# Unequal units at the two ends of a software pipeline, weights loaded after the first gate, and input tiles moved to multiples of 512 B

## The chip, the cores and the metric

The kernel runs on one core of one Trainium2 chip. The metric is the device time in microseconds (us). The core has six units that matter here: TensorE (PE in the profile; PEld is its weight load), VectorE (DVE), ScalarE (ACT), GpSimd (POOL), SyncE (SP, here only an issuer of transfers) and 16 DMA engines.

A reported time is about 2 us longer than the span of the profile of the same run (237.56 against 235.8 us for the profiled run of the kernel before). Each run also lists the mean clock that TensorE was granted. The times of one kernel move a little with it: the kernel before took 235.8 us in a run at 0.998, 236.2 at 0.992 and 237.7 at 0.984. I therefore say the clock where a difference of one us matters.

## The reference

Four sequences of 6336 steps, 256 channels: a gated recurrence, then a highway layer on its result.

```python
sig = 1 / (1 + exp(-f_logit));  f = lb + (1 - lb) * sig;  i = 1 - f
h = f[:, t] * h + i[:, t] * x[:, t]          # for t in 0..6335; y[:, t] = h
H = maximum(y @ w_h, 0);  T = 1 / (1 + exp(-(y @ w_t + b_t)))
out = T * H + (1 - T) * y
```

Inputs and outputs are float32. 52.4 MB are read and 25.9 MB written, in whatever way the work is cut.

## The kernel before

The time axis is cut into *units* of columns, a column being one step of one sequence. A unit of 1024 columns is one sequence's piece of 1024 steps; the first unit holds the 192 odd steps of all four sequences (768 columns, on 96 partitions). The units go through a software pipeline, one unit per iteration `n`:

```python
rest = S % (NB * P)                                     # 192
units = [(rest // 2, [(b, 0, b * rest, rest) for b in range(B)])]   # 768 columns
for s0 in range(rest, S, NB * P):
    for b in range(B):
        units.append((P, [(b, s0, 0, NB * P)]))         # 24 units of 1024 columns
...
outp = ctx.enter_context(tc.tile_pool(name="outp", bufs=2))
...
for n in range(-3, NU + 2):
    load(n + 4)                       # SyncE: lt (f_logit) and xt (x)
    z_pe(n - 1, 0); scan(n, 0)        # TensorE; VectorE: y = f*y + b
    t_act(n - 1, 0)                   # ScalarE: t = sigmoid(z)
    o_pe(n - 2, 0); o_act(n - 2, 0)   # TensorE; ScalarE copy o, SyncE output
    decay_pe(n + 1, 0); decay_act(n + 1, 0)   # transposes uT; ScalarE f
    d_dve(n - 1, 0)                   # VectorE d
    ...                               # the same for the second half of channels
    gate(n + 2)                       # ScalarE: u = sigmoid(-f_logit)
    ...
    after = e_dve(n - 1)              # VectorE e = d*t
    product(n + 2, after)             # GpSimd: bv = u*x, held until e is done
# (cut: ok(n) guards, second halves)
```

So one iteration holds the VectorE work of unit `n` (scan) and of unit `n-1` (d, e), and the ScalarE work of units `n+2` (gate), `n+1` (f), `n-1` (t) and `n-2` (copy). Each of the matmul results has a single buffer in PSUM.

## Time and profile before

| | before |
|---|---|
| time, median of the first 3 runs | 236.1 us (235.98 to 236.21) |
| VectorE busy | 203.6 us, 86% of the span |
| ScalarE busy | 198.3 us, 84% |
| TensorE busy | 192.1 us, 81% |
| first scan | 16.48 us |
| one 1024-column unit | 8.19 us |
| end of the last e to the end of the span | 9.0 us |

The page of the kernel before: the span, the busy times, three rows of the 40 slices (digits are tenths, 9 is 90% or more; PEclk is the granted clock), and the chain of waits by engine.

```profile
span 235.8 us, 4853 instructions
PE 192.1 (81%) x2000; PEld 134.5 (57%) x2000; DVE 203.6 (86%) x144; ACT 198.3 (84%) x176; POOL 114.2 (48%) x108
...
DVE  0425799999999999999999999999999999999540
...
PEclk9999999999999999999999999999999999999985
DMA  6999999999999999999999999999999995243255
...
DVE 77%; issue 6%; PE 5%; ACT 2%; DVEq 0%; ACTq 0%
```

VectorE is full from the sixth slice to the last but three; the chain that ended last is 77% VectorE. Only the two ends have room. The timeline of VectorE shows them (columns: start, duration, engine, line, operation, result and operands, shapes, count; in brackets the idle time before and what ended it).

```profile
16.48 1.89 DVE L161 TENSOR_TENSOR_SCAN y<-f,bT 128x192 bf16<-128x192 f16 x4 [5.92 <-PE bT L150]
19.76 1.89 DVE L161 TENSOR_TENSOR_SCAN y<-f,bT 128x192 bf16<-128x192 f16 x4 [1.39 <-PE bT L150]
22.90 2.35 DVE L161 TENSOR_TENSOR_SCAN y<-f,y,bT 128x1024 bf16<-128x1024 f16 x1 [1.26 <-ACT u L119]
...
27.54 2.35 DVE L161 TENSOR_TENSOR_SCAN y<-f,y,bT 128x1024 bf16<-128x1024 f16 x1 [1.39 <-ACT t L183]
...
31.65 2.34 DVE L161 TENSOR_TENSOR_SCAN y<-f,y,bT 128x1024 bf16<-128x1024 f16 x1
...
224.16 1.28 DVE L199 SCALAR_TENSOR_TENSOR d<-y,ncc,gp 128x1024 bf16<-128x1024 bf16 x1 [2.55 <-PE gp L190]
225.55 1.23 DVE L206 TENSOR_TENSOR e<-d,t 128x2048 bf16<-128x2048 bf16 x1
```

Nothing is scanned for 16.5 us, three gaps of 1.3 to 1.4 us follow at the start and one of 2.55 us before the last d, and after the last e (which ends at 226.8) two copies and the last outputs take 9 us more.

Here the granted clock of TensorE falls to half from 228 us on (columns: stretch, its length, then PE, PEld, DVE, ACT, POOL busy with their counts, granted clock, DMA share, GB/s):

```profile
228.00:230.00 2.00, 1.01 (x10) 1.01 (x10) 0.00 (x0) 0.94 (x1) 0.00 (x0) 0.54 0.26 92
230.00:232.00 2.00, 0.85 (x8) 0.58 (x6) 0.00 (x0) 1.01 (x1) 0.00 (x0) 0.50 0.69 245
```

The last 16 matmuls of 128 columns take 308 ns on average there, where those before them took 220.

### The profile page before, as it was taken

Reading aid. Unit: us, or ns where it says so; the run is one execution under the profiler, and the core shown is the slowest. Engines: PE = TensorE matmul, PEld = TensorE weight load, DVE = VectorE, ACT = ScalarE, POOL = GpSimd, SP = SyncE. Lnnn points to the kernel's source line nnn. Section 1 sums busy time; section 2 is a strip of 40 time slices with the busy share of each in tenths; the row PEclk is TensorE's granted clock in tenths of the full one; section 3 lists DMA queues with packets and bytes.
Section 4 is the critical chain, followed back from the end, with each engine's and each line's share of the span. In section 5 each row is a group of like instructions: output and inputs, shape, how many; then the busy total and the mean of one; then the engine's idle time right before and its main releaser. Section 6 shows DMA issues by size and latency. Waiting matters only on the chain.

```text
span 235.8 us, 4853 instructions
## 1 busy us (share of the span) xinstructions
PE 192.1 (81%) x2000; PEld 134.5 (57%) x2000; DVE 203.6 (86%) x144; ACT 198.3 (84%) x176; POOL 114.2 (48%) x108
## 2 busy tenths in 40 slices
PE   0135899898999989899998989898999989897751
PEld 0125566666566666667566666656666666665441
DVE  0425799999999999999999999999999999999540
ACT  0645789999999999999999999999999999975541
POOL 1088553574376357436634753673475357430000
PEclk9999999999999999999999999999999999999985
DMA  6999999999999999999999999999999995243255
GB/s 150 302 386 386 386 383 386 379 385 383 382 386 383 386 382 386 384 384 379 386 386 382 385 383 383 379 382 375 385 383 386 388 368 205 97 152 119 89 178 177
DMA packets 78805, 78.68 MB, mean 334 GB/s; under 512 B 2240, under 2 KB 78784, under 8 KB 78784
## 3 DMA queue, kind: packets, MB, share of 16 engines
q1 hardware_dynamic: 77664, 77.86, 94.4%
q10 hardware_dynamic: 1120, 0.53, 0.9%
q8 instruction: 15, 0.25, 0.4%
q14 instruction: 6, 0.05, 0.0%
HBM read 52.43 MB, written 25.95 MB: 332 GB/s over the span
## 4 chain that ended last, share of the span: by engine, by line
DVE 77%; issue 6%; PE 5%; ACT 2%; DVEq 0%; ACTq 0%
DVE y L161 45%; DVE d L199 20%; DVE e L206 12%; PE zp L175 1%; PE gp L190 1%; ACT o L233 1%; ACT t L183 1%; PE op L224 1%; PE op L223 1%; PE bT L150 0%; PE uT L136 0%; DVE e L209 0%; DVEq L206 0%; ACTq L233 0%; DVEq L209 0%
## 5 line engine op out<-in xcount | busy, mean ns | idle before, releaser
L126 POOL TENSOR_TENSOR bv<-u,xt 128x512 bf16<-128x512 f16 (+1 forms) x100 | 113.2, 1164 | 93.7 <-DVE e L206 72.9
L161 DVE TENSOR_TENSOR_SCAN y<-f,y,bT 128x1024 bf16<-128x1024 f16 x48 | 112.3, 2341 | 2.6 <-ACT t L183 1.4
L183 ACT ACTIVATE t<-zp,bt 128x1024 bf16<-128x1024 f32 (+1 forms) x50 | 55.3, 1106 | 13.6 <-PE zp L175 10.6
L199 DVE SCALAR_TENSOR_TENSOR d<-y,ncc,gp 128x1024 bf16<-128x1024 bf16 (+1 forms) x50 | 62.2, 1244 | 2.5 <-PE gp L190 2.5
L144 ACT ACTIVATE f<-uT,ncc 128x1024 f16<-128x1024 f16 (+1 forms) x50 | 55.9, 1117 | 5.5 <-PE uT L136 5.5
L233 ACT COPY o<-op 128x1024 f32<-128x1024 f32 (+1 forms) x50 | 50.2, 1005 | 5.7 <-PE op L224 5.7
L190 PE MATMUL gp<-y,w_sb 128*128 128x512 bf16 (+1 forms) x200 | 51.5, 380 | 4.0 <-DVE d L199 1.4
L223 PE MATMUL op<-diag,y 128*128 128x128 f16 (+1 forms) x400 | 50.9, 221 | 2.2 <-ACT o L233 2.2
L175 PE MATMUL zp<-y,w_sb 128*128 128x512 bf16 (+1 forms) x200 | 51.6, 381 | 0.3 <-ACT t L183 0.3
L224 PE MATMUL op<-ident_b,e 128*128 128x128 bf16 (+1 forms) x400 | 50.8, 221 | 0.5 <-DVE e L206 0.5
L119 ACT ACTIVATE u<-lt 128x2048 f16<-128x2048 f32 (+1 forms) x25 | 47.5, 1902 | 2.1 <-DMA lt<-in_f_logit_dram 2.1
L150 PE MATMUL bT<-ident_b,bv 128*128 128x128 bf16 (+1 forms) x400 | 31.7, 222 | 20.8 <-DVE y L161 16.5
L224 PEld LDWEIGHTS <-e 128*128 128x128 bf16 (+1 forms) x400 | 39.7, 100 | 8.8 <-DVE e L206 1.9
L223 PEld LDWEIGHTS <-y 128*128 128x128 bf16 (+1 forms) x400 | 39.8, 100 | 5.7
L150 PEld LDWEIGHTS <-bv 128*128 128x128 bf16 (+1 forms) x400 | 26.8, 99 | 27.5 <-issue 20.0
L136 PE MATMUL uT<-ident_h,u 128*128 128x128 f16 (+1 forms) x400 | 32.2, 227 | 11.0 <-ACT u L119 10.0
L190 PEld LDWEIGHTS <-w_sb 128*128 128x128 f16 x200 | 19.6, 98 | 24.4 <-issue 7.1
L136 PEld LDWEIGHTS <-u 128*128 128x128 f16 (+1 forms) x400 | 26.0, 103 | 11.4 <-ACT u L119 10.0
L206 DVE TENSOR_TENSOR e<-d,t 128x2048 bf16<-128x2048 bf16 x24 | 29.4, 1225 | 2.9 <-DVE d L199 0.5
L175 PEld LDWEIGHTS <-w_sb 128*128 128x128 f16 x200 | 18.7, 99 | 18.2 <-issue 1.1
L161 DVE TENSOR_TENSOR_SCAN y<-f,bT 128x192 bf16<-128x192 f16 x8 | 3.8, 534 | 7.3 <-PE bT L150 7.3
L119 ACT ACT_TABLE_LOAD x1 | 1.3, 1283 | 6.7 <-DMA lt<-in_f_logit_dram 6.7
(15 smaller groups left out, 5.7 us busy)
## 6 DMA issues: line engine op xcount, KB each, us to landing
lt<-in_f_logit_dram SPq DMA_DIRECT2D x24, 1024.0 KB, 9.3
xt<-in_x_dram SPq DMA_DIRECT2D x24, 1024.0 KB, 10.6
out_dram<-o SPq DMA_DIRECT2D x48, 512.0 KB, 7.9
lt<-in_f_logit_dram SPq DMA_DIRECT2D x2, 384.0 KB, 5.0
xt<-in_x_dram SPq DMA_DIRECT2D x2, 384.0 KB, 5.7
out_dram<-o SPq DMA_DIRECT2D x2, 384.0 KB, 6.6
w_raw<-in_moe_w_h_dram ACTq DMA_DIRECT2D x1, 256.0 KB, 4.8
w_raw<-in_moe_w_t_dram ACTq DMA_DIRECT2D x1, 256.0 KB, 5.4
```

What stands on the lines that cost most here:

```text
L126: ins = pin(nc.gpsimd.tensor_mul(bv[:np_, q:q + 2], st[n]["u"][:np_, q:q + 2], st[n]["xt"][:np_, q:q + 2]))
L136: pin(nc.tensor.transpose(uT[:, j * np_:(j + 1) * np_], st[n]["u"][:np_, j, h * P:(h + 1) * P], ident_h[:np_, :np_]))
L144: pin(nc.scalar.activation(st[n]["f"][:, h, :N], st[n]["uT"][:, :N], AF.Identity, scale=ncc[:, h:h + 1], bias=1.0))
L150: pin(nc.tensor.transpose(bT[:, j * np_:(j + 1) * np_], st[n]["bv"][:np_, j, h * P:(h + 1) * P], ident_b[:np_, :np_]))
L161: pin(nc.vector.tensor_tensor_scan(y[:, h, c0:c0 + ln], st[n]["f"][:, h, c0:c0 + ln], st[n]["bT"][:, c0:c0 + ln], 0.0 if prev is None else ...
L175: pin(nc.tensor.matmul(zp[:, i, :e - a], w_sb[:, 1, ki, m * P:(m + 1) * P], y[:, ki, a:e], start=ki == 0, stop=ki == NH - 1))
L183: pin(nc.scalar.activation(st[n]["t"][:, m, :, :w], st[n]["zp"][:, :, :w], AF.Sigmoid, bias=bt[:, m:m + 1]))
L190: pin(nc.tensor.matmul(gp[:, i, :e - a], w_sb[:, 0, ki, m * P:(m + 1) * P], y[:, ki, a:e], start=ki == 0, stop=ki == NH - 1))
L199: pin(nc.vector.scalar_tensor_tensor(st[n]["d"][:, m, :, :w], y2, ncc[:, m:m + 1], st[n]["gp"][:, :, :w], op0=ALU.mult, op1=ALU.max))
L206: ins = pin(nc.vector.tensor_mul(e, st[n]["d"], st[n]["t"]))
L223: pin(nc.tensor.matmul(o, y[:, h, j * np_:(j + 1) * np_], diag[:, h], start=True, stop=False))
L224: pin(nc.tensor.matmul(o, e[:, h, i, c:c + np_], ident_b, start=False, stop=True))
```

## The change

The intent: start the scan sooner with a small first unit, keep the last unit short so that little stands behind its e, get the weights out of the way of the first loads, and let the input tiles start at multiples of 512 B.

- Units: 256 columns (64 steps of four sequences, loaded as two halves of 64 partitions), 512 (128 steps of four), 512 + 512, then 22 of 1024, and 512 + 256 + 256 for the last one. 29 units instead of 25, the same 25,344 columns.
- The weights (0.5 MB) are loaded by ScalarE after the first gate instead of at its very start; the VectorE work on them stands between the scans of the first two units.
- A small activation at the top loads ScalarE's table before the data come (1.28 us; in the kernel before from 6.71, when lt had landed). Its tile, `warm`, is 256 B a partition; the first input tile moves from 48.5 x 512 B to 49 x 512 B.

```diff
+    FIRST, LAST = (4, 4), (4, 2, 2)
-    units = [(rest // 2, [(b, 0, b * rest, rest) for b in range(B)])]
+    units.append((2, [(b, b * H, H) for b in range(B)],
+                  [(b0, slice(b0, B, 2), 0, b0 * H) for b0 in range(2)]))
+    units.append((4, [(b, b * P, P) for b in range(B)], [(0, slice(0, B), H, 0)]))
...
+            for nb in (LAST if last else FIRST if not b and s0 == H + P else (NB,)):
+                units.append((nb, [(b, 0, nb * P)], [(b, a)]))
+                a += nb * P
...
+    warm = singles.tile([P, 64], FP32, name="warm")
+    nc.gpsimd.memset(warm, 0.0)
+    nc.scalar.activation(warm, warm, AF.Sigmoid)
...
+    def load_weights():
+        for k, w in enumerate((moe_w_t, moe_w_h)):
+            pin(nc.scalar.dma_start(w_raw[:, 1 - k], w.rearrange("(h p) o -> p h o", p=P)))
...
         if ok(n):
             scan(n, 1)
+        if n == 0:
+            weights()
...
+        if n + 2 == 0:
+            load_weights()
```

(Every helper takes the unit's own width instead of a fixed one; e is one instruction for every unit; the output of a unit of up to 512 columns is one copy.)

More of the change, by code (lines that the diff above doesn't have):

```diff
@@ L42 @@
     NB = 8
+    FIRST, LAST = (4, 4), (4, 2, 2)
     out_bsd = out.rearrange("(b s) d -> b s d", b=B)
-    rest = S % (NB * P)
-    assert rest % 2 == 0 and rest // 2 <= P and B * 2 == NB
-    units = [(rest // 2, [(b, 0, b * rest, rest) for b in range(B)])]
-    for s0 in range(rest, S, NB * P):
-        for b in range(B):
-            units.append((P, [(b, s0, 0, NB * P)]))
+    units = []
+    H = P // 2
+    assert S % (NB * P) == H + P and B == 4
+    units.append((2, [(b, b * H, H) for b in range(B)],
+                  [(b0, slice(b0, B, 2), 0, b0 * H) for b0 in range(2)]))
+    units.append((4, [(b, b * P, P) for b in range(B)], [(0, slice(0, B), H, 0)]))
+    for s0 in range(H + P, S, NB * P):
+        for b in range(B):
+            last = s0 + NB * P == S and b == B - 1
+            a = s0
+            for nb in (LAST if last else FIRST if not b and s0 == H + P else (NB,)):
+                units.append((nb, [(b, 0, nb * P)], [(b, a)]))
+                a += nb * P
     NU = len(units)
@@ L65, in pin, with pieces @@
         return tc.keep_in_program_order(ins)
+    def pieces(n, dram, t):
+        nb, _, parts = units[n]
+        if len(parts[0]) == 2:
+            b, a = parts[0]
+            return [(dram[b, a:a + nb * P, :].rearrange("(j p) d -> p j d", p=P), t[:, :nb])]
+        w = H if len(parts) == 2 else P
+        return [(dram[bs, a:a + w, :].rearrange("b p d -> p b d"), t[p0:p0 + w, :nb]) for _, bs, a, p0 in parts]
     def load(n):
-        np_, segs = units[n]
         lt = inp.tile([P, NB, D], FP32, tag="lt")
@@ L71, in load @@
         for src, t in ((f_logit, lt), (x, xt)):
-            if len(segs) == 1:
-                b, s0, _, ln = segs[0]
-                pin(nc.sync.dma_start(t, src[b, s0:s0 + ln, :].rearrange("(j p) d -> p j d", p=np_)))
-            else:
-                t4 = t.rearrange("p (b j) d -> p b j d", j=2)
-                for j in range(2):
-                    nc.sync.dma_start(
-                        t4[:np_, :, j, :],
-                        src[:, j * np_:(j + 1) * np_, :].rearrange("b p d -> p b d"))
-        st[n]["lt"], st[n]["xt"] = lt, xt
+            for dram, sb in pieces(n, src, t):
+                pin(nc.sync.dma_start(sb, dram))
+        st[n]["lt"], st[n]["xt"] = lt, xt
+    warm = singles.tile([P, 64], FP32, name="warm")
+    nc.gpsimd.memset(warm, 0.0)
+    nc.scalar.activation(warm, warm, AF.Sigmoid)
+    lb = singles.tile([P, NH], FP32, name="lb")
+    bt = singles.tile([P, NH], FP32, name="bt")
+    w_raw = singles.tile([P, 2, NH, D], FP32, name="w_raw")
+    nc.scalar.dma_start(lb, lower_bound.rearrange("(h p) -> p h", p=P))
     load(0)
@@ L89 @@
     make_identity(nc, ident_h)
-    lb = singles.tile([P, NH], FP32, name="lb")
-    bt = singles.tile([P, NH], FP32, name="bt")
-    w_raw = singles.tile([P, 2, NH, D], FP32, name="w_raw")
-    for h in range(NH):
-        for vec, t in ((lower_bound, lb), (moe_b_t, bt)):
-            nc.scalar.dma_start(t[:, h:h + 1], bass.AP(
-                tensor=vec.tensor, offset=vec.offset + h * P, ap=[[1, P], [1, 1]]))
-    for k, w in enumerate((moe_w_h, moe_w_t)):
-        nc.scalar.dma_start(w_raw[:, k], w.rearrange("(h p) o -> p h o", p=P))
     cc = singles.tile([P, NH], FP32, name="cc")
@@ L107, with weights @@
     for h in range(NH):
-        for k in range(2):
-            nc.vector.tensor_scalar(w_sb[:, k, h], w_raw[:, k, h], cc[:, h:h + 1], None, op0=ALU.mult)
         nc.vector.tensor_scalar(diag[:, h], ident_h, cc[:, h:h + 1], None, op0=ALU.mult)
         nc.vector.tensor_scalar(ndiag[:, h], ident_h, ncc[:, h:h + 1], None, op0=ALU.mult)
-        nc.vector.scalar_tensor_tensor(w_sb[:, 0, h, h * P:(h + 1) * P], w_raw[:, 0, h, h * P:(h + 1) * P],
-                                       cc[:, h:h + 1], ndiag[:, h], op0=ALU.mult, op1=ALU.add)
+    def load_weights():
+        for k, w in enumerate((moe_w_t, moe_w_h)):
+            pin(nc.scalar.dma_start(w_raw[:, 1 - k], w.rearrange("(h p) o -> p h o", p=P)))
+        pin(nc.scalar.dma_start(bt, moe_b_t.rearrange("(h p) -> p h", p=P)))
+    def weights():
+        for h in range(NH):
+            pin(nc.vector.tensor_scalar(w_sb[:, :, h], w_raw[:, :, h], cc[:, h:h + 1], None, op0=ALU.mult))
+            pin(nc.vector.scalar_tensor_tensor(
+                w_sb[:, 0, h, h * P:(h + 1) * P], w_raw[:, 0, h, h * P:(h + 1) * P], cc[:, h:h + 1], ndiag[:, h],
+                op0=ALU.mult, op1=ALU.add))
     def gate(n):
-        np_, _ = units[n]
+        nb = units[n][0]
         u = inp.tile([P, NB, D], FP16, tag="u")
-        pin(nc.scalar.activation(u[:np_], st[n]["lt"][:np_], AF.Sigmoid, scale=-1.0))
+        pin(nc.scalar.activation(u[:, :nb], st[n]["lt"][:, :nb], AF.Sigmoid, scale=-1.0))
         st[n]["u"] = u
     def product(n, after):
-        np_, _ = units[n]
         bv = mid.tile([P, NB, D], BF16, tag="bv")
-        for q in range(0, NB, 2):
-            ins = pin(nc.gpsimd.tensor_mul(bv[:np_, q:q + 2], st[n]["u"][:np_, q:q + 2], st[n]["xt"][:np_, q:q + 2]))
+        for q in range(0, units[n][0], 2):
+            ins = pin(nc.gpsimd.tensor_mul(bv[:, q:q + 2], st[n]["u"][:, q:q + 2], st[n]["xt"][:, q:q + 2]))
             if q == 0 and after is not None:
@@ L132, in decay_pe @@
     def decay_pe(n, h):
-        np_, _ = units[n]
         uT = ps1.tile([P, NB * P], FP16, tag="uT")
-        for j in range(NB):
-            pin(nc.tensor.transpose(uT[:, j * np_:(j + 1) * np_], st[n]["u"][:np_, j, h * P:(h + 1) * P], ident_h[:np_, :np_]))
+        for j in range(units[n][0]):
+            pin(nc.tensor.transpose(uT[:, j * P:(j + 1) * P], st[n]["u"][:, j, h * P:(h + 1) * P], ident_h))
         st[n]["uT"] = uT
     def decay_act(n, h):
-        np_, _ = units[n]
-        N = NB * np_
+        N = units[n][0] * P
         if h == 0:
@@ L146, in b_pe @@
     def b_pe(n, h):
-        np_, _ = units[n]
         bT = ps1.tile([P, NB * P], BF16, tag="bT")
-        for j in range(NB):
-            pin(nc.tensor.transpose(bT[:, j * np_:(j + 1) * np_], st[n]["bv"][:np_, j, h * P:(h + 1) * P], ident_b[:np_, :np_]))
+        for j in range(units[n][0]):
+            pin(nc.tensor.transpose(bT[:, j * P:(j + 1) * P], st[n]["bv"][:, j, h * P:(h + 1) * P], ident_b))
         st[n]["bT"] = bT
@@ L158, in scan @@
         y = st[n]["y"]
-        for b, _, c0, ln in units[n][1]:
+        for b, c0, ln in units[n][1]:
             prev = carry.get((b, h))
@@ L164, in scan, with spans @@
             carry[b, h] = y[:, h, c0 + ln - 1:c0 + ln]
-    def halves(n):
-        N = NB * units[n][0]
-        return [(0, N // 2), (N // 2, N)]
+    def spans(n):
+        N = units[n][0] * P
+        return [(a, min(a + 512, N)) for a in range(0, N, 512)]
     def z_pe(n, m):
-        zp = ps1.tile([P, 2, 512], FP32, tag="zp")
-        y = st[n]["y"]
+        zp = ps1.tile([P, NB * P], FP32, tag="zp")
         for ki in range(NH):
-            for i, (a, e) in enumerate(halves(n)):
-                pin(nc.tensor.matmul(zp[:, i, :e - a], w_sb[:, 1, ki, m * P:(m + 1) * P], y[:, ki, a:e],
-                                 start=ki == 0, stop=ki == NH - 1))
+            for a, e in spans(n):
+                pin(nc.tensor.matmul(zp[:, a:e], w_sb[:, 1, ki, m * P:(m + 1) * P], st[n]["y"][:, ki, a:e],
+                                     start=ki == 0, stop=ki == NH - 1))
@@ L177, in z_pe @@
         st[n]["zp"] = zp
     def t_act(n, m):
-        w = NB * units[n][0] // 2
+        N = units[n][0] * P
         if m == 0:
-            st[n]["t"] = ffn.tile([P, NH, 2, 512], BF16, tag="t", name="t")
-        pin(nc.scalar.activation(st[n]["t"][:, m, :, :w], st[n]["zp"][:, :, :w], AF.Sigmoid, bias=bt[:, m:m + 1]))
+            st[n]["t"] = ffn.tile([P, NH, NB * P], BF16, tag="t", name="t")
+        pin(nc.scalar.activation(st[n]["t"][:, m, :N], st[n]["zp"][:, :N], AF.Sigmoid, bias=bt[:, m:m + 1]))
@@ L185, in g_pe @@
     def g_pe(n, m):
-        gp = ps1.tile([P, 2, 512], FP32, tag="gp")
-        y = st[n]["y"]
+        gp = ps1.tile([P, NB * P], FP32, tag="gp")
         for ki in range(NH):
-            for i, (a, e) in enumerate(halves(n)):
-                pin(nc.tensor.matmul(gp[:, i, :e - a], w_sb[:, 0, ki, m * P:(m + 1) * P], y[:, ki, a:e],
-                                 start=ki == 0, stop=ki == NH - 1))
+            for a, e in spans(n):
+                pin(nc.tensor.matmul(gp[:, a:e], w_sb[:, 0, ki, m * P:(m + 1) * P], st[n]["y"][:, ki, a:e],
+                                     start=ki == 0, stop=ki == NH - 1))
@@ L192, in g_pe @@
         st[n]["gp"] = gp
     def d_dve(n, m):
-        w = NB * units[n][0] // 2
+        N = units[n][0] * P
         if m == 0:
-            st[n]["d"] = ffn.tile([P, NH, 2, 512], BF16, tag="d", name="d")
-        y2 = st[n]["y"][:, m, :2 * w].rearrange("p (i w) -> p i w", i=2)
-        pin(nc.vector.scalar_tensor_tensor(st[n]["d"][:, m, :, :w], y2, ncc[:, m:m + 1], st[n]["gp"][:, :, :w],
-                                       op0=ALU.mult, op1=ALU.max))
+            st[n]["d"] = ffn.tile([P, NH, NB * P], BF16, tag="d", name="d")
@@ L202, in e_dve @@
+        pin(nc.vector.scalar_tensor_tensor(st[n]["d"][:, m, :N], st[n]["y"][:, m, :N], ncc[:, m:m + 1],
+                                           st[n]["gp"][:, :N], op0=ALU.mult, op1=ALU.max))
     def e_dve(n):
-        w = NB * units[n][0] // 2
-        e = mid.tile([P, NH, 2, 512], BF16, tag="e", name="e")
-        if w == 512:
-            ins = pin(nc.vector.tensor_mul(e, st[n]["d"], st[n]["t"]))
-        else:
-            for m in range(NH):
-                ins = pin(nc.vector.tensor_mul(e[:, m, :, :w], st[n]["d"][:, m, :, :w], st[n]["t"][:, m, :, :w]))
+        N = units[n][0] * P
@@ L210, in e_dve @@
+        e = mid.tile([P, NH, NB * P], BF16, tag="e", name="e")
+        ins = pin(nc.vector.tensor_mul(e[:, :, :N], st[n]["d"][:, :, :N], st[n]["t"][:, :, :N]))
         st[n]["e"] = e
         return ins
+    QB = NB // 2
     def o_pe(n, q):
-        np_, _ = units[n]
-        w = NB * np_ // 2
-        op = ps1.tile([P, NB // 2, D], FP32, tag="op")
+        op = ps1.tile([P, QB, D], FP32, tag="op")
         y, e = st[n]["y"], st[n]["e"]
-        for jj in range(NB // 2):
-            j = q * (NB // 2) + jj
-            i, c = divmod(j * np_, w)
+        for j in range(q * QB, min((q + 1) * QB, units[n][0])):
@@ L221, in o_pe @@
             for h in range(NH):
-                o = op[:np_, jj, h * P:(h + 1) * P]
-                pin(nc.tensor.matmul(o, y[:, h, j * np_:(j + 1) * np_], diag[:, h], start=True, stop=False))
-                pin(nc.tensor.matmul(o, e[:, h, i, c:c + np_], ident_b, start=False, stop=True))
+                o = op[:, j - q * QB, h * P:(h + 1) * P]
+                pin(nc.tensor.matmul(o, y[:, h, j * P:(j + 1) * P], diag[:, h], start=True, stop=False))
+                pin(nc.tensor.matmul(o, e[:, h, j * P:(j + 1) * P], ident_b, start=False, stop=True))
@@ L225, in o_pe @@
         st[n]["op"] = op
     def o_act(n, q):
-        np_, segs = units[n]
         if q == 0:
             st[n]["o"] = outp.tile([P, NB, D], FP32, tag="o", name="o")
+        j0, j1 = q * QB, min((q + 1) * QB, units[n][0])
         o = st[n]["o"]
-        oq = o[:, q * (NB // 2):(q + 1) * (NB // 2)]
-        pin(nc.scalar.copy(oq[:np_], st[n]["op"][:np_]))
-        if len(segs) == 1:
-            b, s0, _, ln = segs[0]
-            a = s0 + q * (ln // 2)
-            nc.sync.dma_start(out_bsd[b, a:a + ln // 2, :].rearrange("(j p) d -> p j d", p=np_), oq)
-        elif q == 1:
-            o4 = o.rearrange("p (b j) d -> p b j d", j=2)
-            for j in range(2):
-                nc.sync.dma_start(out_bsd[:, j * np_:(j + 1) * np_, :].rearrange("b p d -> p b d"),
-                                  o4[:np_, :, j, :])
+        pin(nc.scalar.copy(o[:, j0:j1], st[n]["op"][:, :j1 - j0]))
@@ L244, in ok @@
+        for dram, sb in pieces(n, out_bsd, o):
+            if len(units[n][2][0]) == 2:
+                dram, sb = dram[:, j0:j1], sb[:, j0:j1]
+            nc.sync.dma_start(dram, sb)
     def ok(n):
@@ L274 @@
             gate(n + 2)
-        if ok(n - 2):
+        if n + 2 == 0:
+            load_weights()
+        if ok(n - 2) and units[n - 2][0] > QB:
             o_pe(n - 2, 1)
```

## The prediction

> **What bounds it now.** In the middle VectorE does. The chain of waits is 77% VectorE (scan 45%, d 20%, e 12%), and one 1024-column unit follows the other every 8.19 us (e starts at 55.07, 63.26); VectorE is busy 39.5 us of each 40.. The DMA engines are never empty either (386 GB/s in every slice from 12 to 190 us; 3.15 MB per 8.19 us unit is 384 GB/s), but loads lead: unit 8's lt, issued at 48.4, lands in 9.3 us; its gate runs near 69. So 24.75 units' worth of columns cost about 203 us of VectorE whatever the split, and only the two ends can shrink. Timeline: first scan at 16.48, gaps of 5.9, 1.4, 1.3 and 1.4 us up to 28 us; last e ends at 226.8 and 9.0 us of outputs follow.
>
> **Start.** The first gate waited until 6.71 for lt, then for 1.28 us of table load, and ran 1.91 us; product waited for xt until 11.46, then ran 4.52 us. After: table load hoisted; unit 0 is 256 columns, 0.5 MiB instead of 1.5. [...] Estimates: lt 5.0, gate 0.6 us, xt 6, product 1.2, first scan near 8. But weights now leave ScalarE after the first gate (5.6 to 7.1); they took 4.8 to 5.4 us to land before, so they land near 11; their VectorE work (about 1.8 us) now stands between the first two units, moving the second to about 13. Three units at 4 to 4.7 us each (half of 8.19 plus a gap) put the first 1024-column scan at about 27. Before, 22.9 with only 768 columns scanned; after, 1792 columns scanned and 1280 finished, 9.2 us more work done in 4.1 us more time, and later gaps of 2.8 us go too: gain 8 us.
>
> **End.** Units of 512, 256, 256: after the last e only four blocks of PE (0.3), one 512-column copy (0.6) and one 256 KB DMA (3.5) stand instead of 9.0: gain 4.4. PE and ScalarE are exposed in the short units: about 0.5 us more gaps than before's 3.0. Four more units cost 0.5.
>
> **Alignment.** The input tiles start 256 B past a multiple of 512 now. [...] a rate above 386 would show in the early slices. With VectorE gapless in the middle it earns nothing there, but it guards the lead: at 386 GB/s xt of the first 1024-unit lands at about 21.5, its scan can start at 26.5, so loads and VectorE are nearly level.
>
> Sum: 236.1 - 8 - 4.4 + 0.5 + 0.5 = **224.7 us**, range 220 to 230. Faster by over 2%: 0.93; within: 0.05; slower: 0.02.
>
> **To see.** First scan at 7 to 9.5; weights' VectorE work delaying the second unit's scans; first 1024-column scan at 25 to 29; 8.19 us per unit unchanged; last e to end 4 to 5 us.
>
> **What would make it wrong.** The lead lost: VectorE waits for product or gate on xt or lt in the middle; weights landing after 14; slow narrow DMAs; SyncE blocked by an output ahead of a load; fewer gaps at the start (220).

About 1.3 us for loading the first unit as halves of 64 partitions were charged in the estimates for the start (lt 5.0, xt 6) and so stand inside the 8. In the kernel after the first gate had its lt at 4.53 us and the first product its xt at 5.77; the halves (128 KB each) took 2.8 us (median) to land. No run loads the same 128 KB over 128 partitions, so whether halves cost more is not shown. The 3.5 us for a 256 KB output were an estimate; the two of the kernel after took 2.1 us. And the slices of the kernel before show 375 to 388 GB/s from 12 to 190 us, not 386 in every one.

## The result, and the profile after

| | before | after |
|---|---|---|
| median of the runs of one job | 236.16 us (4 runs, 235.98 to 236.34) | 232.66 us (4 runs, 232.47 to 233.31) |
| ratio of fast runs, 95% interval | | 0.9857 [0.9836, 0.9878] |
| span of the profile | 235.8 us (a run of 237.56, clock 0.984) | 231.4 us (a run of 233.31, clock 0.999) |

A ratio is the mean time of one kernel's fast runs over the mean time of the other's fast runs of the same rounds, so it is not quite the ratio of the medians. The kernel became 1.4% faster, which is within 2%, where 4.8% had been predicted.

The page after:

```profile
span 231.4 us, 4896 instructions
PE 192.1 (83%) x1967; PEld 133.7 (58%) x1992; DVE 208.1 (90%) x167; ACT 200.3 (87%) x198; POOL 113.3 (49%) x108
...
DVE  1276999999999999999999999999999999999961
...
PEclk9999999999999999999999999999999999999999
DMA  4999999999999999999999999999999999752563
...
DVE 50%; DMA 23%; ACT 9%; PE 9%; issue 6%; SPq 0%; DVEq 0%; ACTq 0%
```

VectorE is full one slice sooner and stays full longer, but it also has 4.5 us more to do (208.1 against 203.6 us, 167 instructions instead of 144). The chain that ended last now passes through transfers for 23% of the span (19% are outputs). The timeline of VectorE after:

```profile
7.49 0.82 DVE L177 TENSOR_TENSOR_SCAN y<-f,bT 128x64 bf16<-128x64 f16 x4 [3.52 <-PE bT L166]
10.74 0.82 DVE L177 TENSOR_TENSOR_SCAN y<-f,bT 128x64 bf16<-128x64 f16 x4 [2.43 <-PE bT L166]
12.60 0.58 DVE L130 TENSOR_SCALAR w_sb<-w_raw,cc 128x512 f16<-128x512 f32 x1 [1.04 <-DMA w_raw<-in_moe_w_h_dram]
...
14.26 1.59 DVE L177 TENSOR_TENSOR_SCAN y<-f,y,bT 128x128 bf16<-128x128 f16 x4
...
19.01 1.27 DVE L177 TENSOR_TENSOR_SCAN y<-f,y,bT 128x512 bf16<-128x512 f16 x1
...
22.78 1.28 DVE L177 TENSOR_TENSOR_SCAN y<-f,y,bT 128x512 bf16<-128x512 f16 x1 [1.85 <-PE bT L166]
...
25.41 1.27 DVE L177 TENSOR_TENSOR_SCAN y<-f,y,bT 128x512 bf16<-128x512 f16 x1
...
29.46 1.38 DVE L218 TENSOR_TENSOR e<-d,t 128x1024 bf16<-128x1024 bf16 x1
30.76 2.33 DVE L177 TENSOR_TENSOR_SCAN y<-f,y,bT 128x1024 bf16<-128x1024 f16 x1
...
37.30 0.69 DVE L218 TENSOR_TENSOR e<-d,t 128x1024 bf16<-128x1024 bf16 x1 [0.45 <-ACT t L198]
37.91 2.34 DVE L177 TENSOR_TENSOR_SCAN y<-f,y,bT 128x1024 bf16<-128x1024 f16 x1
...
225.85 0.48 DVE L212 SCALAR_TENSOR_TENSOR d<-y,ncc,gp 128x256 bf16<-128x256 bf16 x1 [0.87 <-PE gp L204]
226.44 0.42 DVE L218 TENSOR_TENSOR e<-d,t 128x512 bf16<-128x512 bf16 x1
```

The first scan came nine us sooner, but the scan of the first 1024-column unit came only at 30.76. To compare kernels with different units, count the columns that have been scanned:

| moment | before | after | gain |
|---|---|---|---|
| first scan starts | 16.48 | 7.49 | 9.0 |
| 1792 columns scanned (next scan starts) | 31.65 | 30.76 | 0.9 |
| 2816 columns scanned | 39.84 | 37.91 | 1.9 |
| 24,320 columns scanned (the last 1024 begin) | 212.16 | 210.81 | 1.4 |
| last e ends | 226.8 | 226.9 | -0.1 |
| span ends | 235.8 | 231.4 | 4.4 |

The gain of the start has shrunk to 1.9 us before the steady state begins, the middle loses 0.6 (172.3 us from 2816 to 24,320 columns before, 172.9 after), and the end wins 3.0. (The trace of before is of a run 1.4 us over its median, so the gain of the medians is 3.5, not 4.4.) Two of these figures belong to the two profiled runs and not to the kernels: e1 below, the same kernel up to a padding, takes 172.3 us in the middle, and about 1.0 of the 3.0 us is the half clock at the end of the trace before.

### The profile page after: what moved, and what is told of

The parts are those of the page before. It is cut to its first block, busy times and chain, and to the rows that moved or that the text cites. A ratio compares the mean times of both kernels' runs of the same rounds, so it can differ in the third digit from the quotient of the medians.

```text
span 231.4 us, 4896 instructions
## 1 busy us (share of the span) xinstructions
PE 192.1 (83%) x1967; PEld 133.7 (58%) x1992; DVE 208.1 (90%) x167; ACT 200.3 (87%) x198; POOL 113.3 (49%) x108
## 4 chain that ended last, share of the span: by engine, by line
DVE 50%; DMA 23%; ACT 9%; PE 9%; issue 6%; SPq 0%; DVEq 0%; ACTq 0%
DVE y L177 29%; DMA out_dram<-o 19%; DVE d L212 12%; DVE e L218 8%; DMA w_raw<-in_moe_w_h_dram 3%; ACT o L239 3%; ACT t L198 2%; ACT f L161 2%; ACT u L139 2%; PE gp L204 2%; PE zp L190 2%; PE op L231 2%; PE op L230 2%; DMA lt<-in_f_logit_dram 1%; PE bT L166 1%
## 5 line engine op out<-in xcount | busy, mean ns | idle before, releaser
L145 POOL TENSOR_TENSOR bv<-u,xt 128x512 bf16<-128x512 f16 x99 | 112.1, 1162 | 104.8 <-DVE e L218 69.7
L177 DVE TENSOR_TENSOR_SCAN y<-f,y,bT 128x1024 bf16<-128x1024 f16 (+3 forms) x62 | 116.8, 1892 | 3.6 <-PE bT L166 3.2
L198 ACT ACTIVATE t<-zp,bt 128x1024 bf16<-128x1024 f32 (+2 forms) x58 | 57.6, 993 | 8.6 <-PE zp L190 7.5
L212 DVE SCALAR_TENSOR_TENSOR d<-y,ncc,gp 128x1024 bf16<-128x1024 bf16 (+2 forms) x58 | 63.8, 1100 | 1.1 <-PE gp L204 1.1
L161 ACT ACTIVATE f<-uT,ncc 128x1024 f16<-128x1024 f16 (+2 forms) x58 | 58.0, 1001 | 2.8 <-PE uT L154 2.8
L230 PE MATMUL op<-diag,y 128*128 128x128 f16 x396 | 50.4, 220 | 3.2 <-ACT o L239 2.7
L139 ACT ACTIVATE u<-lt 128x2048 f16<-128x2048 f32 (+2 forms) x29 | 48.2, 1661 | 5.1 <-DMA lt<-in_f_logit_dram 5.1
L231 PE MATMUL op<-ident_b,e 128*128 128x128 bf16 x396 | 50.1, 220 | 1.0 <-DVE e L218 1.0
L231 PEld LDWEIGHTS <-e 128*128 128x128 bf16 x396 | 38.8, 98 | 12.2 <-issue 4.3
L230 PEld LDWEIGHTS <-y 128*128 128x128 bf16 x396 | 38.9, 98 | 5.9 <-issue 0.3
```

The lines of the kernel that those rows point to most:

```text
L145: ins = pin(nc.gpsimd.tensor_mul(bv[:, q:q + 2], st[n]["u"][:, q:q + 2], st[n]["xt"][:, q:q + 2]))
L161: pin(nc.scalar.activation(st[n]["f"][:, h, :N], st[n]["uT"][:, :N], AF.Identity, scale=ncc[:, h:h + 1], bias=1.0))
L177: pin(nc.vector.tensor_tensor_scan(y[:, h, c0:c0 + ln], st[n]["f"][:, h, c0:c0 + ln], st[n]["bT"][:, c0:c0 + ln], 0.0 if prev is None else ...
L198: pin(nc.scalar.activation(st[n]["t"][:, m, :N], st[n]["zp"][:, :N], AF.Sigmoid, bias=bt[:, m:m + 1]))
L212: pin(nc.vector.scalar_tensor_tensor(st[n]["d"][:, m, :N], st[n]["y"][:, m, :N], ncc[:, m:m + 1], st[n]["gp"][:, :N], op0=ALU.mult, op1=AL ...
L230: pin(nc.tensor.matmul(o, y[:, h, j * P:(j + 1) * P], diag[:, h], start=True, stop=False))
```

## The experiments

Seventeen kernels ran; each is an edit of the kernel after unless said otherwise. All gave the right result except e7. All numbers are medians of all runs in us, with the ratio to the kernel before of the same job. e1 to e4 shared one job with e1 equal to the kernel after up to a padding, so e1's 232.70 serves there as "after". The kernel after itself (232.66) ran in a job of its own; that e1 repeats it within 0.1 us says how well jobs compare, but a difference of half a us between jobs stays doubtful. A run is called slow when it is over 1.5% above the fastest of its kernel. One run of e9 and one of e13 are; the ratios leave them out.

### The alignment: e1

```diff
-    warm = singles.tile([P, 64], FP32, name="warm")
+    warm = singles.tile([P, 128], FP32, name="warm")[:, :64]
```

> The changed kernel with 256 B of padding, so that all large SBUF tiles start 256 B past a multiple of 512 again, as before. If the start address matters to transfers, the rate in the slices with loads alone (386 GB/s in both kernels) falls below 383 and the time rises by 1 us or more. My theory, from equal rates before and after: no effect, 386 GB/s and within 0.5 us of the changed kernel's 232.7.

Measured: 232.70, ratio 0.9835 [0.9797, 0.9873]. In the three slices from 12 to 29 us the kernel before (tiles 256 B past a multiple of 512) shows 386, 386 and 386 GB/s and the kernel after 382, 386 and 386; the rate of e1 itself is not on record. The tiles' start at a multiple of 512 B has no effect that these runs show, as predicted.

### Which end earns what: e2, e8, e10, e15

```diff
-    FIRST, LAST = (4, 4), (4, 2, 2)
+    FIRST, LAST = (4, 4), (NB,)         # e2
+    FIRST, LAST = (NB,), (4, 2, 2)      # e8
+    FIRST, LAST = (4, 4), (4, 4)        # e15
```

> The changed kernel with its last 1024 columns as one unit again. The comparison of the two traces says that the split end gives about 3 us; so 235.5 expected (range 234.5 to 236.5). If the rival holds (transfers bound the kernel, so the end cannot give much), it stays under 233.7.

Measured: 234.88, ratio 0.9933 [0.9894, 0.9973], so 2.2 us over e1. The short units of the end are worth 2.2 us, and everything else together 236.22 - 234.88 = 1.3 us. The traces agree: from the start of the last 1024 columns to the end e2 takes 22.6 us and e1 20.6.

> The changed kernel with the first full 1024 columns as one unit instead of two of 512 (the units of 256, 512 and the split end stay). By fixed costs alone it would be 0.5 us faster; but the first 1024-column product (4.5 us instead of 2.3) must then end before its scan, so VectorE idles for up to 2 us. Expected within 1 us of the changed kernel: 232.7 to 233.7 if the split pays, 232.0 to 232.5 if it only costs.

Measured: 232.82, ratio 0.9841 [0.9805, 0.9878], the same as the kernel after. With the first full unit whole, VectorE waits 1.49, 1.51 and 2.20 us for the transposes bT, but saves the cost of one cut. That cut earns nothing that is clear of the noise.

e10 merges the first two units into one of 768 columns on all 128 partitions, and leaves the first full unit whole; the rest (table load, weights, the end) is as after.

> The changed kernel with its first two units (256 and 512 columns) made one unit of 768 on all 128 partitions, and the first 1024 whole: the sizes at the start are then those of before, all else as changed. If the small first units are what pays at the start, this is 2 us or more slower (234.7 or more). If their fixed costs and the uneven sizes eat what they win (my theory since the six mid splits cost 2.5 us each), within 0.8 us of the changed kernel (231.9 to 233.5).

Measured: 234.06, ratio 0.989 [0.9859, 0.992], between the two expectations. First scan at 13.02, 1792 columns scanned at 31.55. So the small first units, for all that they start 5.5 us sooner, are worth only about 1.4 us (234.06 against 232.66).

> The last full unit is cut into 512 + 512 instead of 512 + 256 + 256; nothing else differs from the kernel after. The split of the end was worth about 2.2 us against a whole last unit (e2_last_whole). Theory A (each further cut costs VectorE about 0.6 us and saves about as much of the tail: one 256 KB output instead of one of 512 KB): within 0.5 us of the kernel after, 232.2 to 233.2. Rival B (most of the gain of the end comes from the very last 256-column piece): 233.5 or more.

Measured: 233.02, ratio 0.9878 [0.985, 0.9907], 0.4 us over the kernel after. Most of the gain of the end is in the first cut. That the last one adds anything is not shown: the runs of the two kernels overlap (232.68 to 233.92 and 232.47 to 233.31), and in the traces the last 1024 columns take 20.4 us to the end, against 20.6.

### What a cut costs: e4, e12, e14

```diff
-            for nb in (LAST if last else FIRST if not b and s0 == H + P else (NB,)):
# e4: six units of the third sequence, far apart, get FIRST
# e12: every full unit but the last gets FIRST (22 more units)
# e14: six units that follow one another get FIRST
```

> The changed kernel with six more of its 1024-column units (those of the third batch row) cut into two of 512, in the middle where VectorE has no gaps. Theory (fixed cost per VectorE instruction): a scan of 512 starts 1.19 us before the next instruction against 2.26 for 1024, d 0.65 to 0.7 against 1.17, e 0.62 against 1.14, so five more instructions cost about 0.5 us a split: 3 us in all, 235.7 (range 234.7 to 237). If an extra unit costs only the 0.1 us that the prediction assumed, under 233.4.

Measured: 247.51, ratio 1.0468 [1.0422, 1.0513], 14.8 us over e1: 2.5 us a cut, far from the 0.5 that was expected. The busy time of each engine in two stretches of e4 (columns: stretch, its length, then PE, PEld, DVE, ACT, POOL busy with their counts, granted clock, DMA share, GB/s); the first line is the iteration in which VectorE has the two 512-column halves, the second the next one:

```profile
79.47:84.82 5.35, 4.23 (x62) 3.59 (x62) 4.58 (x7) 5.33 (x7) 4.53 (x4) 1.00 1.02 341
84.82:92.59 7.77, 5.41 (x64) 3.84 (x62) 6.57 (x6) 7.77 (x9) 4.53 (x4) 1.00 1.03 327
```

ScalarE is busy for 5.33 of 5.35 and for 7.77 of 7.77 us, while VectorE has only 4.58 and 6.57 us of work. A short unit shortens VectorE's part of its own iteration, but ScalarE's gate, f and copy of that iteration belong to neighbours of full length. That made a theory: it is the *uneven neighbours* that cost, not the cut.

> The changed kernel with every 1024-column unit but the last cut into two of 512: 22 more units than in the changed kernel, but all of one size. If the 2.5 us that each of the six mid splits cost is a fixed cost of one more unit, 22 x 2.5 = 55 us: 285 or more. If most of it came from uneven neighbours and only the 1.1 us of VectorE's fixed costs is a unit's own, 22 x 1.1 = 24 us: 254 to 262.

Measured (one round): 246.32, ratio 1.0405 [1.0352, 1.0459], 13.7 us over the kernel after for 22 more units: 0.62 us each, less than either expectation. In its middle a 512-column unit takes 4.45 us (e at 100.72, 105.17, 109.62), where half of 8.19 is 4.10.

> Six 1024-column units that follow one another (indices 10 to 15 of the full units) are cut into 512 + 512: the same six extra units as in e4_split_mid, which cost 14.8 us there, 2.5 us each. Theory A (the cost of a split is mostly that of an uneven neighbour, a ScalarE gate of 1024 columns in an iteration whose VectorE d and e are of 512): only two edges remain instead of twelve, so 6 x 0.62 us (the price of a split in e12_all512) and about 1.9 us for the edges: 236.5 to 240, near 238.5. Theory B (each split costs 2.5 us of itself wherever it stands): 246 to 249 as e4. Within the run of 512-column units the trace should show about 4.45 us a unit with ScalarE never 100% busy for a whole unit.

Measured: 241.23, ratio 1.0171 [1.0125, 1.0218], 8.6 us over the kernel after with the same six extra units that cost 14.8 in e4. One stretch within the run of short units, and one at its far edge, where 1024-column units come back:

```profile
127.20:131.66 4.46, 3.79 (x40) 2.61 (x41) 4.36 (x6) 4.29 (x7) 2.29 (x2) 1.00 1.09 385
...
154.43:161.64 7.21, 4.80 (x52) 3.22 (x51) 4.44 (x5) 5.56 (x7) 4.52 (x4) 1.00 1.09 383
```

Inside, VectorE is full (4.36 of 4.46 us) and a cut costs 2 x 4.455 - 8.19 = 0.72 us. At the edges VectorE waits for 0.74 us going in and 3.77 us coming out. 6 x 0.72 + 4.5 = 8.8 us, the measured 8.6. The theory holds in direction, since neighbours decide most of the price, but the size at the edge was underrated: 241.2 lies over its range of 236.5 to 240. ScalarE's copies waited there for output transfers too (1.01, 1.65 and 0.80 us), so the far edge is not the gate's length alone.

### Is it the transfers? e5, e7

```diff
-    outp = ctx.enter_context(tc.tile_pool(name="outp", bufs=2))
+    outp = ctx.enter_context(tc.tile_pool(name="outp", bufs=3))     # e5
+            if q == 1 and 8 <= n < 22: continue                     # e7: no output
```

> The changed kernel with three output tiles instead of two. In its trace ScalarE's copies wait 4.4 us in six places for an output transfer to land, and between 177 and 194 us the units take 8.45 and 8.89 us instead of 8.19. Theory A: that costs about 1 us, so 0.3 to 1.2 us faster (231.5 to 232.4). Rival B (transfers are the ceiling): the copies no longer wait but VectorE then waits for loads, and the time stays within 0.2 us.

Measured: 232.20, ratio 0.9804 [0.9768, 0.984]. The gap at 37 us is gone, which the two-tile traces of the kernel after, e1 and e11 have (0.45, 0.56 and 0.65 us). The gaps at 184 to 190 us are gone too, but they were not the two tiles' doing: e1 has two tiles and no such gaps, and its middle takes 172.3 us as in e5 and in the kernel before. The gain is about 0.5 us (232.20 against 232.66); it fits the gap at 37 us, but as a difference between jobs it is at the edge of what can be seen.

> Wrong result on purpose: the changed kernel without the second half of the output transfer of 14 units in the middle (7 MB of the 26 MB written), all else the same. If transfers are the ceiling (rival B), 7.3 MB at 386 GB/s are worth up to 19 us and the time falls by 3 us or more. Theory A (VectorE is the ceiling in the middle): only the waits of copies for landing outputs go, 0 to 1.2 us.

Measured: 232.44, ratio 0.982 [0.9776, 0.9863], hardly faster with 14 outputs of 512 KB less. The transfers are not the ceiling of the middle.

### The weights: e6, e11

```diff
+    load_weights()      # on SyncE: e6 between load(0) and load(1), e11 after load(1)
-        if n + 2 == 0:
-            load_weights()
```

> The changed kernel with the weights issued on SyncE's queue between the loads of the first and second units instead of on ScalarE's queue after the first gate. They should land near 8 instead of 12.5; the second unit's first scan, held to 14.26 by the weights' VectorE work, can start at about 13.5 when its product ends. Theory A: 0.5 to 1.2 us faster (231.5 to 232.2). Rival: the second unit's lt, now 1.4 us later, delays its gate and the start stays as it is (within 0.3 us).

Measured: 235.93, ratio 0.9972 [0.9925, 1.0019], 3.3 us *slower* and outside both expectations. The weights landed 3.4 us after their issue instead of 6.5 to 7.5, but they took the place of lt of the next unit (issued at 5.15 us instead of 3.48), so its gate (10.45 instead of 8.36) and everything in order behind it on ScalarE came later. VectorE's work on the weights, from 13.56 us on, fell beside GpSimd's product (11.89 to 14.17 and 14.66 to 17.16): its four instructions took 0.89, 0.35, 1.38 and 1.13 us, where they took 0.58, 0.35, 0.48 and 0.35 in the kernel after. An e of the kernel after shows the same: 1.38 us at 29.46, beside a product (25.77 to 30.29), and 0.69 at 37.30, without one.

```profile
12.83 0.82 DVE L178 TENSOR_TENSOR_SCAN y<-f,bT 128x64 bf16<-128x64 f16 x4 [3.82 <-PE bT L167]
...
16.18 1.13 DVE L133 SCALAR_TENSOR_TENSOR w_sb<-w_raw,cc,ndiag 128x128 f16<-128x128 f32 x1
17.23 1.58 DVE L178 TENSOR_TENSOR_SCAN y<-f,y,bT 128x128 bf16<-128x128 f16 x4
```

> The changed kernel with the weights on SyncE's queue after the loads of the second unit, so that they no longer share the engines with xt of that unit. xt then should land near 9.3 instead of 10.6, the weights near 11; the second unit's first scan at 12.5 to 13.4 instead of 14.26, and 0.6 to 1.4 us faster (231.3 to 232.1). If the time does not move (within 0.3 us), a start 1 us earlier is lost again before the even stretch, as in the run with TensorE kept busy.

Measured: 233.13, ratio 0.9858 [0.9824, 0.9892], the same as the kernel after. The second unit's scan moved from 14.26 to 12.91, but its second half waited 1.27 us for its transposes, and the first 1024-column scan stayed where it was (30.7). (What the expectation calls sharing the engines is, in the kernel after, that the weights, issued at 4.54 and 5.01 us and landing 6.5 and 7.5 us later, were on the way together with xt of the second unit, issued at 4.12 and waited for until 10.62.)

### TensorE at half speed: e3, e9, e13, e16, e17

The groups of matmuls by shape, in two stretches of the kernel after, first 14 to 22.4 us, then 23 to 31 us (busy us, mean ns of one):

```profile
L154 PE MATMUL uT<-ident_h,u 128*128 128x128 f16 x12 | 1.9, 314 | 0.0
```

```profile
L154 PE MATMUL uT<-ident_h,u 128*128 128x128 f16 x20 | 1.6, 219 | 0.0
```

The same transposes take 314 ns, then 219. Started back to back they follow each other at about 107 and 56 ns. TensorE ran at half speed until 22.4 us, although the row of the granted clock shows 9 throughout. It was not idle in that time: transposes included, it was busy for 2.35, 2.10 and 2.95 of 3 us in the stretches 14 to 17, 17 to 20 and 20 to 23 us. The wait of 1.85 us at 20.9 falls into this time, and is as large as the whole gain of the start (1.9). e3 gives TensorE junk matmuls while it would wait. They write into the PSUM buffer of the outputs, which is not needed yet:

```diff
+    FILL = {("d", 0, 0): 36, ("b", 0, 0): 16, ("d", 1, 0): 28, ("b", 1, 0): 18}
+    def fill(*key):
+        k = FILL.get(key, 0)
+        if k:
+            junk = ps1.tile([P, NB // 2, D], FP32, tag="op", name="junk")
+        for _ in range(k):
+            pin(nc.tensor.matmul(junk[:, 0, :P], ident_h, ident_h, start=True, stop=True))
```

> The changed kernel with about 100 unused 128-wide matmuls put into TensorE's idle time before the first, second and third transposes, writing PSUM that nothing reads. In the changed kernel every matmul before 22.4 us takes about 1.4 to 1.7 times what it takes later (128 wide: 314 against 219 ns mean, 107 against 56 ns from start to start). Theory A (the half-speed TensorE is part of what ate the gain at the start): the gap of 1.85 us before the scan at 22.78 shrinks below 0.8 and the kernel is 1 to 2.5 us faster (230.2 to 231.7). Rival B (transfers are the ceiling; time won at the start is paid back later): the first 1024-column scan starts earlier, but the end moves by under 0.5 us.

Measured: 233.72, ratio 0.9867 [0.9823, 0.9911], 1.0 us slower than e1: a miss. The first 1024-column scan did come 1.5 us sooner (29.26), but then ScalarE's copy stood still:

```profile
34.62 1.01 ACT L250 COPY o<-op 128x1024 f32<-128x1024 f32 x1 [3.31 <-DMA out_dram<-o]
```

It waited 3.31 us for an output tile. SyncE issues the outputs in order with the loads (in the kernel after an xt at 22.61 us, two outputs from 25.28 on, the next lt at 28.59), an output of 512 KB takes 7.9 us to land here (median), and there are two tiles. The next unit's scan came at 37.87, against 37.91 in the kernel after: all that was won had been given back. Then more was lost. TensorE had little to do while the copy stood (it was busy for 1.36 of 3 us from 32 to 35), its granted clock fell to 0.50 from 37.2 to 40.6 us, and VectorE waited for it once more:

```profile
42.62 2.35 DVE L188 TENSOR_TENSOR_SCAN y<-f,y,bT 128x1024 bf16<-128x1024 f16 x1 [1.23 <-PE bT L177]
```

Nor did the filling do all of its work: the clock was at half from 16.7 to 20.1 us as well, and the gap that should have shrunk below 0.8 us still was 1.17. e9 joins e3 and e5.

> The two earlier edits together: TensorE kept busy at the start and three output tiles. With TensorE kept busy alone, the first full scan of 1024 came 1.5 us earlier (29.26 against 30.76), and then ScalarE stood 3.31 us for the transfer of an output tile, so the next unit's scan came at 37.87, no earlier than in the changed kernel (37.91). Theory A: with a third tile the 1.5 us stay: next unit's scan near 36 and 0.8 to 1.6 us faster than the changed kernel with three tiles (230.6 to 231.4). Rival B (transfers as a whole hold the start): the wait only moves to a load, and it stays at 232 to 232.5.

Measured: 232.18 (231.96 without the slow run), ratio 0.9789 [0.9743, 0.9835]. The median lies in or just under the rival's range, but the runs are mixed: 230.09 in one at clock 1.000, 231.9 to 232.5 in those at 0.978 to 0.985. In its profiled run (0.978) TensorE was back at half speed from 15.4 to 22.2 us, the granted clock there 0.5, and VectorE waited 1.83 us as without the filling. e13 fills more places (34, 16, 28, 24, 12 and 18 matmuls at six places) and keeps the third tile.

> Junk matmuls at more places at the start than in e9_pe_out3, to keep TensorE at full speed through the first units, and a third output tile. Theory A (TensorE's half-speed start and the wait of the copy for an output tile both hold the start, and each hides the other): 128-wide matmuls near 220 ns by 15 us in the profiled run, first 1024-column unit starts at about 29, the next unit's scan at about 36 (37.9 in the kernel after, 37.2 with the third tile alone), time 230 to 231.2. Rival B (the start is held by weights, ScalarE and VectorE alone): next unit's scan at 37 or later, time 231.8 to 232.7 as e5_out3.

Measured: 230.90 over all six runs, 230.38 over the five fast ones, ratio 0.972 [0.9675, 0.9766], faster than both kernels. (The kernel before ran mostly at clock 0.984 in this job, 237.7, which flatters the ratio; against the 232.66 of the kernel after it is 0.8 to 1.0%.) Its runs at clock 0.993 to 0.995 took 229.5 to 230.4 us, those at 0.985 and 0.986 took 231.4 and 232.2 (the slow one was at 0.972). VectorE in the profiled run:

```profile
14.51 1.59 DVE L188 TENSOR_TENSOR_SCAN y<-f,y,bT 128x128 bf16<-128x128 f16 x4
...
19.06 1.27 DVE L188 TENSOR_TENSOR_SCAN y<-f,y,bT 128x512 bf16<-128x512 f16 x1
...
23.51 1.27 DVE L188 TENSOR_TENSOR_SCAN y<-f,y,bT 128x512 bf16<-128x512 f16 x1
...
29.05 2.33 DVE L188 TENSOR_TENSOR_SCAN y<-f,y,bT 128x1024 bf16<-128x1024 f16 x1
...
33.78 2.35 DVE L188 TENSOR_TENSOR_SCAN y<-f,y,bT 128x1024 bf16<-128x1024 f16 x1 [1.75 <-PE bT L177]
...
37.47 2.34 DVE L188 TENSOR_TENSOR_SCAN y<-f,y,bT 128x1024 bf16<-128x1024 f16 x1
```

With the transposes at 219 ns up to 29 us, the three short units took 14.5 us (14.51 to 29.05), where they took 16.5 in the kernel after and 14 in the prediction. In this run, however, TensorE fell back to half speed at 29.5 us, where the page's row of the clock now shows it, and the next second half waited 1.75 us:

```profile
PEclk9999979999999999999999999999999999999997
```

So theory A's first number came (29.05 for 29) and its second did not (37.47 for 36); in e17 below, which had no fall-back there, it came too (36.05). The spread of the runs fits a fall-back that happens in some of them, but only one run is profiled.

> e13_pe_full_out3 with the first 1024-column unit not split. Theory A (the split there costs 0.6 to 2.5 us and no longer buys anything once TensorE is warm): 229 to 231, at or under e13. Rival B (the small unit still covers the load of the first full unit): 0.5 to 1.5 us over e13.

Measured: 232.10, ratio 0.9785 [0.9752, 0.9818], 1.2 us over e13 (1.7 over its fast runs), which is in the rival's range. Without the cut, ScalarE's gate of the first full unit waited 3.43 us for a 1 MB lt, and VectorE 3.93 us for transposes behind it. But the rival is not shown. In the traces e16 has 1792 and 2816 columns scanned at 28.97 and 37.16 us, no later than e13 with its fall-back (29.05 and 37.47). And all its runs were at 0.981 to 0.989; e13's two runs at such a clock took 231.4 and 232.2, as long as these. Clock and cut are not separated.

e17 is e13 with e11's place for the weights.

> e13_pe_full_out3 (junk matmuls at the start, third output tile) with the weights loaded on SyncE after the loads of unit 1, as in e11_w_after1 (on the kernel after that edit moved the second unit's scan from 14.26 to 12.91 and won nothing). Theory A (the weights' late landing is a term of its own, about 1.3 us of the miss, that shows once TensorE is at full speed): the second unit's scan near 13, the first 1024-column scan near 27.8 (29.05 in e13), time 228.5 to 230.2. Rival B (the weights only take the place of lt of unit 2 in the queue, which lands later and makes ScalarE's gate late): first 1024-column scan at 28.7 or later, time 230.4 to 231.4 as e13.

Measured: 230.93, ratio 0.9779 [0.9742, 0.9816], the same time as e13 within the spread of the runs (229.43 to 232.47).

```profile
13.01 1.59 DVE L189 TENSOR_TENSOR_SCAN y<-f,y,bT 128x128 bf16<-128x128 f16 x4
...
16.40 1.59 DVE L189 TENSOR_TENSOR_SCAN y<-f,y,bT 128x128 bf16<-128x128 f16 x4 [1.43 <-PE bT L178]
...
29.25 2.33 DVE L189 TENSOR_TENSOR_SCAN y<-f,y,bT 128x1024 bf16<-128x1024 f16 x1
...
36.05 2.34 DVE L189 TENSOR_TENSOR_SCAN y<-f,y,bT 128x1024 bf16<-128x1024 f16 x1
```

The second unit starts 1.5 us sooner than in e13 and loses 1.43 us at once; the first 1024-column scan is at 29.25, against 29.05. Ahead of that wait stood a gate that waited 1.98 us for its lt, and 12 of my own junk matmuls, at half clock (1.34 us). The two were not separated, so whether an earlier landing of the weights could be kept stays open. What is shown is that neither of the two places on SyncE's queue wins time.

## Why the prediction was wrong

The bound, the shape of both ends and most of the marks were right: VectorE bounds the middle and its 8.19 us per unit did not change; the first scan came at 7.49 (7 to 9.5); the weights' work did stand in front of the second unit; the alignment earned nothing; from the last e to the end took 4.5 us (4 to 5). Which line failed is "Three units at 4 to 4.7 us each (half of 8.19 plus a gap) put the first 1024-column scan at about 27", with the "gain 8 us" built on it. Of 8, 1.9 us arrived (1.3 by e2, which compares medians). Point by point:

| term of the sum | predicted | measured | difference |
|---|---|---|---|
| second unit's scan (weights landed at 12.5, not 11) | 13 | 14.26 | 1.3 |
| three short units, to the first 1024-column scan | 14.0 | 16.5 | 2.5 |
| wait in the next unit (gone in e5) | 0 | 0.45 | 0.45 |
| a gap of before counted twice (the 1.26 before 22.90) | | | 1.3 |

1. **The three short units.** They took 4.75, 6.40 and 5.35 us. Most of the excess is TensorE at half speed until 22.4 us, a wait of 1.85 us in one place. This is shown by e13: with the matmuls at 219 ns the same stretch took 14.5 us. e9 is the check on it: it has the third tile and junk matmuls too, but TensorE at half speed from 15.4 to 22.2 us, and the stretch took 16.5 us (13.98 to 30.45). So 2.0 of the 2.5 us are TensorE's. I had read the durations of matmuls in the steady state only; the kernel before has the same slow matmuls until 26.7 us (311 ns for uT), and I did not look.
2. **The weights.** They took 6.5 and 7.5 us to land, not the 4.8 to 5.4 of before; they were issued at 4.5 and 5.0 us, behind the loads of two units and among those of the third. That delay is in the trace. That it costs time of its own is *not* shown: in e11 and e17 the unit moved by 1.4 and 1.5 us and the gain was lost within the next half.
3. **A bookkeeping error.** The 4.1 us between 22.9 and 27 already contained one of the gaps that "go too"; 1.3 us were counted twice.
4. With the wait of 0.45 us in the next unit, gone in e5, these make 5.5 of the 6.1 us that are missing. The last 0.6 I cannot assign.

The other small step that failed is "Four more units cost 0.5". The price of a cut is 0.62 to 0.72 us among equals (e12, e14) and 2.5 us alone among 1024-column units (e4). The fixed cost could be read from the trace before: a d of 1024 columns took 1.255 us and one of 768 took 0.988, that is, as an estimate from the two, 1.04 ns a column and 0.19 us for each instruction. The trace after shows the same: 2 x 724 - 1256 = 192 ns for d and 2 x 1276 - 2341 = 211 ns for a scan of 512 columns. Each cut adds two scans, two d and one e on VectorE, and I charged 0.125 us. At the end this shows too: the way from last e to the end shrank by 4.5 us, as predicted (4.4), but from the start of the last 1024 columns to the last e the kernel took 16.1 us instead of 14.6, so 3.0 us remain in the traces, where 4.4 - 0.5 = 3.9 was predicted, and 2.2 us by e2. The two differ because the 9.0 us from which the prediction counted held about 1.0 us of half clock: a figure of one profiled run (237.56 us) was taken off the median of others (236.1).

A pattern connects these: at the start every engine waits in turn, and a wait that is taken away uncovers the next one. e3 brought the first 1024-column scan 1.5 us forward and met the wait for an output tile (3.31 us); e11 and e17 took away 1.4 us of the weights' and met a late gate. The two removals together gained more than either: e5 alone 0.5 us, e3 alone lost 1.0, e13 and e17 (third tile and fuller filling) won 1.7 to 2.3 us (230.93, and 230.90 or 230.38 in fast runs, against 232.66). The fuller filling without the third tile was not run, so how much of this needs the tile is not shown.

What stays open: whether the weights' late landing costs anything of itself, the last 0.6 us of the start, and what exactly sends TensorE back to half speed. On the last the traces say something. The spells of half clock at the start of e3, e9, e13, e16 and e17 last 3.4 us each (6.8 in e9), worked out from the granted clock of stretches of 3 us. In the last whole stretch of 3 us before each fall TensorE was busy for 1.3 to 2.0 us (1.74 and 1.36 in e3, 1.34 in e9, 1.33 in e13, 1.97 in e16, 1.77 in e17), and up to 41 us none with more than 2.0 came right before one. But six stretches with 1.26 to 1.82 us (one in e3, two in e13, one in e16, two in e17) had no fall in them or in the next. So the junk matmuls did not keep TensorE busy where it fell back; the exact condition is not shown.

## What to carry to other kernels

Cutting the first and last units of a software pipeline wins only what the *slowest* engine of each shortened iteration lets through: count the work of every unit that shares the iteration, not of the short one alone, and keep short units next to short ones, because here a lone cut cost 2.5 us and a cut among equals 0.7. Before you cost the start with durations of the steady state, read the durations of the start itself. When one wait is taken away and nothing comes of it, look for the buffer or queue that was hidden behind it, and try the two removals together.
